# Three more 512-token blocks through the Strassen loop of a two-mixer kernel, with their combined weights formed beside attention

## The chip, the cores and the metric

One core of a Trainium2 chip runs the program. The metric is device microseconds of one execution. Before the change the median of three runs is 1919.4 us (1916.83 to 1920.06).

## What is computed

```python
# attention: q, k, v are (8, 8, 576, 64); k and v are averaged over 8 neighbours first
scores = q @ k_p.T / sqrt(64);  x = softmax(scores) @ v_p        # -> (8, 576, 512)
# first mixer: token mixing of rank 32, then a channel network 512 -> 2048 -> 512
u = x + (x.T @ U @ V).T
x = u + relu(u @ w_ch1) @ w_ch2
# second mixer: 2-D Fourier transform (real part), layer norm, a channel network of the same size
u = x + real(fft(fft(x, axis=1), axis=2))
out = u + relu(norm(u) @ w_ch1b) @ w_ch2b
```

There are 4608 tokens of 512 channels in 8 batches of 576. All is float32; every operand of a large product is split into a high and a low part, and a product is three matmuls (high by high, high by low, low by high).

## The kernel before

The two channel networks take nearly all of TensorE's time. Each has a first product (512 to 2048 channels, in 16 column blocks f of 128) and a second one (2048 back to 512).

**First mixer** (lines 1097 to 1171). Tokens come in groups of 256 (`T`); the first two run as a pair. For each f, `st1` (L879) makes one [128, 256] tile of the hidden layer and `st2` (L927) multiplies the tile of an earlier f by `W[1, f]`. One turn of the f loop is called a slot here; 18 groups of 16 slots cover all tokens, the first two groups sharing their slots. In each slot other work, written as Python generators ("lanes", L1017), moves on by a step: attention (`a`), the rank-32 mixing (`mix`), loads (`prep`), weights (`w`), operands of the next group (`p`), and the spectral work (`d`).

`st1` has two forms. As long as attention runs (no `Dft` object), a tile takes twelve 128x256 matmuls. Afterwards ("beside", L880) it takes four 128x512 and four 128x256 matmuls with the same number of columns in all.

**Weights.** The raw inputs are float64 bit patterns. `w_first` (L137) converts those of the first mixer to split float32 in `W[0, f]` and `W[1, f]`, with integer operations on VectorE (L124, L129, L130), copies on ScalarE and the subtraction of the split on GpSimd (L100). `w_second` (L177) does it for the second mixer's first matrix and forms the seven combinations of Strassen's scheme (Winograd's form) per pair of column blocks, splits them (`put`, GpSimd again) and stores them in the DRAM tile `wc`; then it converts the second matrix into `wd`. It uses a ring of four `wo` tiles.

**Second mixer** (lines 1207 to 1263). Blocks of 512 tokens (`TA`). For each of 8 pairs p of column blocks, seven `product` calls (L867) of six 128x256 matmuls each replace what would be eight; weights come in pairs through a ring of four slots (`ring_load`, L861, 512 KB each). `st2_a` (L957) is the second product. `prep_a` (L765) makes the operands of a block: it loads four tiles of 128 tokens from `u2d`, normalises them, transposes each with four TensorE matmuls against `ident` (L812) and splits. In the first mixer `turn_prep` (L707) transposes on VectorE instead. Four times in each p, `tick` (L1192) lets the spectral lane, the operands and `swap` move a step.

**Spectral work** (`Dft.run`, L523) handles one batch; the middle rows of several batches are gathered and handled together at the end of a group (`GROUPS`). It starts when all attention and weight lanes are done, runs beside the first mixer until its end and then beside the second, and writes `u2d`. `swap` (L1082) replaces `W[1, f]` by the second mixer's matrix, from the last 16 slots of the first mixer on.

What sets the order: up to the second mixer a scheduler of the language places the instructions of TensorE, VectorE, GpSimd and SyncE by its own estimates and the written order; an instruction whose inputs and buffers are free may be placed well ahead of where it is written. ScalarE keeps the written order from the second group on, TensorE and VectorE from the second mixer on. Every engine and the DMA queue of SyncE then work strictly in the order placed.

## Time and profile before

| | before |
|---|---|
| median of three runs | 1919.4 us |
| the profiled execution, its own time | 1924.2 us |
| its span, first to last instruction | 1922.4 us |
| mean granted TensorE clock | 0.989 |
| TensorE busy | 1840.7 us (96%) |
| VectorE busy | 1024.2 us (53%) |
| ScalarE busy | 676.6 us (35%) |
| GpSimd busy | 173.3 us (9%) |

Start times are in us from the span's start. The first mixer's matmuls begin at 65.7, attention and weight work end at 770, the spectral work runs from 772 to 1541, the second mixer's first product begins at 1088, and the last store is issued at 1919. Matmuls are pipelined, so the difference between the starts of two neighbouring groups, not a matmul's own duration, is what a group costs.

### The profile page before, as it was taken

To read this page: it belongs to the slowest core of one execution; us is meant where nothing else is said; L and a number is where in the kernel's file an instruction comes from. 1 tells how busy PE (TensorE), PEld (TensorE's weight loads), DVE (VectorE), ACT (ScalarE), POOL (GpSimd) and SP (SyncE) were. 2 spreads that over 40 slices of the span, in tenths; PEclk is the share of its full clock that TensorE was granted. 3 is DMA by queue.
4 is the path that set the end of the run, shared out by engine and by line. 5 is a ranking of instruction groups with operands and counts; after the bars stand their busy time and mean duration, and the time that the engine had idled before them with its cause. 6 is when DMAs were issued, how large, how long until landed. Compare 5 with 4: busy or idle time off the path is not lost. (4 is left out here: it accounts for less than half of the span.)

```text
span 1922.4 us, 30977 instructions
## 1 busy us (share of the span) xinstructions
PE 1840.7 (96%) x11252; PEld 1633.1 (85%) x11252; DVE 1024.2 (53%) x2365; ACT 676.6 (35%) x2116; POOL 173.3 (9%) x309
## 2 busy tenths in 40 slices
PE   4789899999999999999999899999999999999999
PEld 3578789898988888888888788899898999999998
DVE  8985464546454444545455855565656454445332
ACT  6553434343433332222232533333333323333221
POOL 3431011111100000100000100000000000000000
PEclk9799999999999999999999999999999999999999
DMA  9535464647453534422223767686768666666564
GB/s 362 173 115 176 134 196 141 196 129 214 120 184 110 144 105 136 131 78 63 77 64 99 247 195 223 214 260 208 223 223 265 201 223 191 229 185 225 182 212 132
DMA packets 255417, 335.63 MB, mean 175 GB/s; under 512 B 84576, under 2 KB 109248, under 8 KB 255264
## 3 DMA queue, kind: packets, MB, share of 16 engines
q1 hardware_dynamic: 254336, 330.25, 54.9%
q0 software_dynamic: 928, 3.40, 0.5%
q8 instruction: 89, 1.46, 0.3%
q14 instruction: 64, 0.52, 0.1%
HBM read 268.69 MB, written 64.88 MB: 174 GB/s over the span
## 5 line engine op out<-in xcount | busy, mean ns | idle before, releaser
L110 PE MATMUL h<-utx,w 128*128 128x256 f32 (+1 forms) x3048 | 479.6, 302 | 14.3 <-DVE hl L921 5.9
L110 PE MATMUL o<-w,hh 128*128 128x512 f32 x1632 | 478.8, 399 | 1.7 <-DVE ur L103 0.8
L110 PEld LDWEIGHTS h<-utx,w 128*128 128x128 f32 x3048 | 432.6, 192 | 55.3 <-DVE hl L921 9.3
L110 PEld LDWEIGHTS h<-x,wr 128*128 128x128 f32 x3024 | 396.2, 191 | 27.2 <-issue 4.8
L110 PE MATMUL h<-x,wr 128*128 128x256 f32 x3024 | 411.4, 284 | 5.9 <-DMA wr<-wc 3.6
L110 PEld LDWEIGHTS o<-w,hh 128*128 128x128 f32 x1632 | 289.4, 190 | 49.1 <-ACT hh L920 2.3
L110 PE MATMUL o<-w,hl 128*128 128x512 f32 x816 | 278.4, 398 | 2.5 <-DVE hl L921 1.6
L110 PEld LDWEIGHTS o<-w,hl 128*128 128x128 f32 x816 | 150.3, 190 | 29.1 <-DVE hl L921 2.9
L103 DVE TENSOR_TENSOR side<-h,side 128x256 f32<-128x256 f32 (+1 forms) x144 | 79.5, 552 | 116.7 <-PE h L110 116.1
L413 ACT ACTIVATE s<-s,mx 128x72 f32<-128x72 f32 x296 | 90.4, 332 | 70.6 <-DVE mx L410 70.1
L915 ACT ACTIVATE low<-h 128x256 f32<-128x256 f32 x102 | 39.1, 383 | 205.3 <-PE h L110 168.4
L1183 ACT ACTIVATE hh<-side 128x256 fp32r<-128x256 f32 (+1 forms) x144 | 75.0, 521 | 94.7 <-DVE side L103 93.3
L920 ACT ACTIVATE hh<-h 128x256 fp32r<-128x256 f32 x170 | 65.6, 386 | 97.3 <-PE h L110 88.8
L1183 ACT ACTIVATE hh<-h 128x256 fp32r<-128x256 f32 x72 | 27.6, 383 | 203.8 <-PE h L110 202.3
L1189 DVE SCALAR_TENSOR_TENSOR hl<-h,hh 128x256 fp32r<-128x256 f32 x72 | 30.4, 423 | 124.4 <-ACT hh L1183 123.3
L103 DVE TENSOR_TENSOR low<-h,low 128x256 f32<-128x256 f32 x102 | 42.9, 420 | 94.1 <-ACT hh L916 91.5
L1189 DVE SCALAR_TENSOR_TENSOR hl<-side,hh 128x256 fp32r<-128x256 f32 (+1 forms) x144 | 79.3, 551 | 22.8 <-ACT hh L1183 21.3
L921 DVE SCALAR_TENSOR_TENSOR hl<-h,hh 128x256 fp32r<-128x256 f32 x170 | 70.4, 415 | 34.6 <-ACT hh L920 34.1
L110 PE MATMUL m<-w,hh 128*128 128x512 f32 x304 | 83.6, 394 | 0.0
L110 PE MATMUL hu<-w,hh 128*128 128x512 f32 x288 | 78.6, 394 | 0.0
L100 POOL TENSOR_TENSOR wo<-wo 128x256 fp32r<-128x256 f32 x56 | 43.3, 784 | 325.9 <-ACT wo L106 309.0
L413 ACT ACTIVATION_READ_ACCUMULATOR s<-s,mx 128x1 f32 x296 | 64.5, 218 | 0.0
(254 smaller groups left out, 2346.0 us busy)
## 6 DMA issues: line engine op xcount, KB each, us to landing
wr<-wc SPq DMA_DIRECT2D x252, 512.0 KB
x<-x SPq DMA_DIRECT2D x56, 256.0 KB
wc<-wo SPq DMA_DIRECT2D x56, 256.0 KB
ur<-ud SPq DMA_DIRECT2D x36, 256.0 KB
x1d<-ur SPq DMA_DIRECT2D x36, 256.0 KB
ul<-u2d SPq DMA_DIRECT2D x36, 256.0 KB
ur<-u2d SPq DMA_DIRECT2D x36, 256.0 KB
out<-ur SPq DMA_DIRECT2D x36, 256.0 KB
```

The source lines that it names most:

```text
L100: eng.tensor_tensor(out=o, in0=a, in1=b, op=ALU.subtract)
L103: eng.tensor_tensor(out=o, in0=a, in1=b, op=ALU.add)
L110: nc.tensor.matmul(o, a, b, start=start, stop=stop, skip_group_check=True)
L413: nc.scalar.activation(out=s[:n, a], in_=v[:, k], func=ACTF.Exp, bias=mx[:n, a:a + 1], accum_out=sm[:n, a:a + 1])
L915: nc.scalar.activation(out=low, in_=o[:, T:2 * T], func=ACTF.Copy)
L920: nc.scalar.activation(out=hh, in_=p, func=ACTF.Relu)
L921: nc.vector.scalar_tensor_tensor(out=hl, in0=p, scalar=0.0, in1=hh.bitcast(F32), op0=ALU.max, op1=ALU.subtract)
L1183: nc.scalar.activation(out=hh[:, i], in_=c, func=ACTF.Relu)
L1189: nc.vector.scalar_tensor_tensor(out=hl[:, i], in0=c, scalar=0.0, in1=hh[:, i].bitcast(F32), op0=ALU.max, op1=ALU.subtract)
```

## The change

The first mixer's own loop ends after 12 groups of 256 tokens. The last three blocks of 512 tokens (`SB` = 6 to 8) go through the Strassen loop ahead of the second mixer's nine, in one sequence `seq` of twelve blocks; a phase number selects the source (`ud` or `u2d`), the destination (`x1d` or `out`), the combined weights (`wc[0]` or `wc[1]`), and whether there is a layer norm.

The new lane `w_combine` forms the first mixer's combinations from `W[0, f]`, which lies in SBUF already split: per pair p eight additions or subtractions of 128x256 on VectorE, four splits (ScalarE, GpSimd), seven stores of 256 KB; `w_second` comes after it, and the `w` lane gets two steps in every second slot. The exchange of `W[1, f]` moves into the Strassen loop, behind the last use by the third block. Spectral groups are four pairs of batches.

```diff
-GROUPS = ((0, 1, 2), (3,), (4, 5), (6, 7))
+GROUPS = ((0, 1), (2, 3), (4, 5), (6, 7))
+SB = 6
...
-    wc = dram.tile([7 * NPR, 128, 512], F32, name="wc")
+    wc = [dram.tile([7 * NPR, 128, 512], F32, name=f"wc{i}") for i in range(2)]
...
+    def w_combine(at):
+
+        def half(p, i, h):
+            return W[0, 2 * p + i].bitcast(F32)[:, :, 256 * h:256 * h + 256]
+
+        def plain(w, n):
+            nc.sync.dma_start(out=wc[0][n].rearrange("p (h x) -> p h x", h=2), in_=w)
+
+        def put(o, n):
+            split(o[:, 0], o[:, 1], o[:, 1].bitcast(F32), nc.gpsimd)
+            nc.sync.dma_start(out=wc[0][n], in_=o.bitcast(F32).rearrange("p h x -> p (h x)"))
+
+        for p in range(NPR):
+            z = 7 * p
+            w11, w12, w21, w22 = half(p, 0, 0), half(p, 1, 0), half(p, 0, 1), half(p, 1, 1)
+            ra, rb, t1, t2 = at.wo(), at.wo(), at.wo(), at.wo()
+            a, b, x, y = ra.bitcast(F32), rb.bitcast(F32), t1.bitcast(F32), t2.bitcast(F32)
+            add(nc.vector, a[:, 0], w11[:, 0], w11[:, 1])
+            add(nc.vector, a[:, 1], w12[:, 0], w12[:, 1])
+            plain(w11, z)
+            yield
+            add(nc.vector, b[:, 0], w22[:, 0], w22[:, 1])
+            add(nc.vector, b[:, 1], w21[:, 0], w21[:, 1])
+            plain(w22, z + 4)
+            yield
+            sub(nc.vector, x[:, 1], a[:, 1], a[:, 0])
+            sub(nc.vector, a[:, 1], b[:, 0], a[:, 1])
+            plain(w21, z + 6)
+            yield
+            sub(nc.vector, y[:, 1], b[:, 0], x[:, 1])
+            sub(nc.vector, b[:, 1], b[:, 1], y[:, 1])
+            yield
+            for o, n in ((t1, 1), (ra, 3), (t2, 2), (rb, 5)):
+                put(o, z + n)
+                yield
...
+    seq = [(0, b) for b in range(SB, NBA)] + [(1, b) for b in range(NBA)]
...
-            nc.sync.dma_start(out=us[t], in_=u2d[r0:r0 + 128, :])
-        ahead = 4 if b else 2
+            nc.sync.dma_start(out=us[t], in_=(ud, u2d)[phase][r0:r0 + 128, :])
+        first = i == 0
+        ahead = 2 if first else 4
...
+            src = wc[seq[2 * m // (7 * NPR)][0]]
...
-            nc.sync.dma_start(out=out[r0:r0 + 128, :], in_=r)
+            nc.sync.dma_start(out=(x1d, out)[phase][r0:r0 + 128, :], in_=r)
+            if not phase and t == 1:
+                state["x1"] = (b + 1) * TA
+        if t == 1 and seq[k] == (0, NBA - 1):
+            swapq.extend((2 * p, 2 * p + 1))
...
-    groups = [[0, 1]] + [[j] for j in range(2, NB)]
+    groups = [[0, 1]] + [[j] for j in range(2, 2 * SB)]
...
-                if "w" not in lanes and not second:
+                if "w" not in lanes and len(second) < 2:
+                    lanes["w"] = (w_combine, w_second)[len(second)](at)
                     second.append(1)
-                    lanes["w"] = w_second(at)
...
-                for name in ("p", "mix", "w", "prep"):
+                for name in ("p", "mix", "w", "prep", "w") if f % 2 else ("p", "mix", "w", "prep"):
...
-    for b in range(NBA):
-        begun = False
+    for k in range(len(seq)):
+        begun = k + 1 == len(seq)
```

How the built order changes is shown at three places.

VectorE at the start, between the conversions of the first mixer's weights (`scr<-wraw`) and the steps that end in the first mixing (`hst`); `wo` is the ring in which combinations are formed. Before:

```order
L433 TENSOR_TENSOR scr_134<-s_430,sm 128x512
L129 SCALAR_TENSOR_TENSOR scr_477<-wraw,scr_477 128x512 x2
L423 TENSOR_SCALAR sm<-sm 128x8
L130 SCALAR_TENSOR_TENSOR scr_477<-wraw,scr_477 128x512 x2
L424 RECIPROCAL sm<-sm 128x8
L124 TENSOR_SCALAR scr_509<-wraw 128x512 x2
L129 SCALAR_TENSOR_TENSOR scr_509<-wraw,scr_509 128x512 x2
L433 TENSOR_TENSOR scr_135<-o_459,sm 128x512
L130 SCALAR_TENSOR_TENSOR scr_509<-wraw,scr_509 128x512 x2
L100 TENSOR_TENSOR hst<-hu,hst 32x512
```

and with the change:

```order
L101 TENSOR_TENSOR wo<-wo 128x256
L372 TENSOR_REDUCE kp<-raw 128x72
L470 TENSOR_TENSOR scr_135<-s_431,sm 128x512
L460 TENSOR_SCALAR sm<-sm 128x8
L130 SCALAR_TENSOR_TENSOR scr_478<-wraw,scr_478 128x512 x2
L101 TENSOR_TENSOR wo<-wo 128x256 x2
L461 RECIPROCAL sm<-sm 128x8
L125 TENSOR_SCALAR scr_510<-wraw 128x512 x2
L131 SCALAR_TENSOR_TENSOR scr_478<-wraw,scr_478 128x512 x2
L101 TENSOR_TENSOR wo<-wo 128x256
L470 TENSOR_TENSOR scr_136<-o_460,sm 128x512
```

Four of the combining operations stand in this piece; eight stand ahead of `hst`, and 40 of all 64 ahead of the last `wraw` conversion.

GpSimd at the same place, where it makes the low parts of `w` and of `wo`. Before:

```order
L100 TENSOR_TENSOR w<-scr_453,w 128x512 x2
L100 TENSOR_TENSOR w<-scr_477,w 128x512 x2
L100 TENSOR_TENSOR w<-scr_509,w 128x512 x2
L100 TENSOR_TENSOR w<-cv,w 128x512
L100 TENSOR_TENSOR w<-scr_684,w 128x512
```

and with the change:

```order
L101 TENSOR_TENSOR w<-scr_454,w 128x512 x2
L101 TENSOR_TENSOR wo<-wo 128x256 x2
L101 TENSOR_TENSOR w<-scr_478,w 128x512
L101 TENSOR_TENSOR wo<-wo 128x256
L101 TENSOR_TENSOR w<-scr_478,w 128x512
L101 TENSOR_TENSOR wo<-wo 128x256
L101 TENSOR_TENSOR w<-scr_510,w 128x512 x2
```

Sixteen of the 32 new subtractions stand ahead of the last one of `w<-cv`.

TensorE, in the first spectral batches. Before, beside the first mixer's slots (`st`: table of the transform, `utx`: operands of 256 tokens):

```order
L110 MATMUL s_8726<-st,xh_8330 128x290 x2
L110 MATMUL s_8726<-st,xl_8331 128x290
L110 MATMUL h_8396<-utx,w 128x512
L110 MATMUL h_8396<-utx,w 128x256
L110 MATMUL h_8396<-utx,w 128x512
L110 MATMUL h_8396<-utx,w 128x256
L110 MATMUL h_8396<-utx,w 128x512
L110 MATMUL h_8396<-utx,w 128x256 x2
L110 MATMUL h_8396<-utx,w 128x512
L110 MATMUL o_8415<-w,hh 128x512 x2
```

and with the change, beside the Strassen loop with the first mixer's tokens (`wr`: ring of combined weights, `x`: combined operands):

```order
L111 MATMUL s_8763<-st,xh_8403 127x290 x2
L111 MATMUL s_8763<-st,xl_8404 127x290
L111 MATMUL s_8763<-st,S 127x290
L111 MATMUL h_8708<-x_8514,wr 128x256 x6
L111 MATMUL h_8709<-x_8517,wr 128x256 x6
L111 MATMUL s_8792<-st,xe_8247 96x290 x2
L111 MATMUL s_8792<-st,xe_8402 96x290 x2
L111 MATMUL s_8792<-st,xe_8589 64x290
L111 MATMUL h_8708<-x_8456,wr 128x256 x6
L111 MATMUL h_8709<-x_8383,wr 128x256 x6
```

In the whole program the order holds, before and now: `h<-utx,w` of 128x512 408 and 72 times, of 128x256 2640 and 2160 times; `h<-x,wr` 3024 and 4032 times; transposes `s<-ident,ul` 128 and 176 times.

## Rows read from the trace of the kernel before

**Rows 1.** Busy time by stretch; columns as in the first line.
```profile
core 0: us, PE busy (x) PEld busy (x) DVE busy (x) ACT busy (x) POOL busy (x), PEclk, DMA share, GB/s
0.00:200.00 200.00, 150.65 (x856) 125.81 (x857) 152.38 (x279) 102.81 (x333) 63.95 (x74) 0.92 0.60 202
200.00:770.00 570.00, 550.68 (x3510) 494.68 (x3509) 285.16 (x664) 217.25 (x848) 48.43 (x74) 0.99 0.51 152
772.00:1000.00 228.00, 227.54 (x1197) 194.78 (x1196) 114.66 (x268) 63.98 (x189) 15.05 (x41) 1.00 0.29 83
1000.00:1110.00 110.00, 103.73 (x566) 87.79 (x565) 74.47 (x191) 42.08 (x116) 10.70 (x22) 1.00 0.55 170
1200.00:1500.00 300.00, 297.95 (x1914) 270.21 (x1912) 172.18 (x426) 98.01 (x250) 23.56 (x69) 1.00 0.71 232
```
**Rows 2.** Timeline of PE, a slot beside the spectral work: start us, us, what.
```profile
902.37 1.57 PE L110 MATMUL h<-utx,w 128*128 128x512 f32 x8
903.78 0.62 PE L110 MATMUL o<-w,hl 128*128 128x512 f32 x2
```
**Rows 3.** Timeline of PE, a slot beside attention.
```profile
400.96 1.58 PE L110 MATMUL h<-utx,w 128*128 128x256 f32 x12
402.38 0.63 PE L110 MATMUL o<-w,hl 128*128 128x512 f32 x2
```
**Rows 4.** Timeline of PE in the Strassen loop, two products and a transpose.
```profile
1704.25 1.59 PE L110 MATMUL h<-x,wr 128*128 128x256 f32 x12
1705.68 1.09 PE L110 MATMUL o<-w,hh 128*128 128x512 f32 x4
...
1707.08 0.60 PE L812 MATMUL s<-ident,ul 128*128 128x128 f32 x4
1707.43 1.67 PE L110 MATMUL h<-x,wr 128*128 128x256 f32 x12
```
**Rows 5.** Busy time in pieces of 20 us at the start.
```profile
40.00:60.00 20.00, 10.48 (x38) 6.42 (x36) 18.31 (x27) 9.76 (x18) 9.34 (x7) 0.73 0.77 297
100.00:120.00 20.00, 15.67 (x79) 13.16 (x80) 19.08 (x31) 11.64 (x33) 10.49 (x7) 0.83 0.41 130
180.00:200.00 20.00, 17.52 (x114) 15.52 (x113) 6.53 (x14) 4.41 (x16) 0.00 (x0) 1.00 0.39 111
```
**Rows 6.** Timeline of DVE ahead of the first mixer's operands; in brackets idle time before.
```profile
53.03 0.69 DVE L100 TENSOR_TENSOR hst<-hu,hst 32x512 fp32r<-32x512 f32 x1 [1.60 <-ACT hst L474]
53.75 1.40 DVE L124 TENSOR_SCALAR cv<-wraw 128x512 int32<-128x512 int32 x1
...
57.71 0.41 DVE L124 TENSOR_SCALAR scr<-wraw 128x512 int32<-128x512 int32 x1
...
64.95 0.68 DVE L100 TENSOR_TENSOR utx<-h,utx 128x512 fp32r<-128x512 f32 x1
```
**Rows 7.** Timeline of PE, the first mixer's first matmuls.
```profile
65.68 1.65 PE L110 MATMUL h<-utx,w 128*128 128x256 f32 x6 [4.04 <-DVE utx L100]
```
**Rows 8.** Timeline of POOL beside rows 6.
```profile
53.59 1.27 POOL L100 TENSOR_TENSOR w<-scr,w 128x512 fp32r<-128x512 f32 x1 [0.76 <-ACT w L106]
```
**Rows 9.** Tile wo on DVE: ns min/median/max, first and last start us.
```profile
L100 DVE TENSOR_TENSOR wo<-wo x32: 380/416/559, 143.2 to 526.6; 128x256 f32<-128x256 f32 x32
```
**Rows 10.** Tile wo on POOL.
```profile
L100 POOL TENSOR_TENSOR wo<-wo x56: 725/740/1184, 143.8 to 532.9; 128x256 fp32r<-128x256 f32 x56
```
**Rows 11.** Tile wraw on DVE.
```profile
L129 DVE SCALAR_TENSOR_TENSOR scr<-wraw,scr x28: 671/680/1775, 21.5 to 124.6; 128x512 int32<-128x512 int32 x28
```
**Rows 12.** Groups of DVE, 30 to 130 us: busy us, mean ns | idle before.
```profile
L129 DVE SCALAR_TENSOR_TENSOR scr<-wraw,scr 128x512 int32<-128x512 int32 x24 | 21.3, 908 | 0.1
```
**Rows 13.** Groups of PE, 200 to 770 us.
```profile
L110 PE MATMUL hu<-xl,ust 128*128 128x512 f32 x30 | 13.1, 437 | 6.0 <-DVE xl L100 5.8
```
**Rows 14.** Groups of PE, 1000 to 1200 us.
```profile
L110 PE MATMUL h<-x,wr 128*128 128x256 f32 x386 | 53.3, 285 | 4.8 <-DMA wr<-wc 2.5 <-DVE side L103 1.4 <-ACT side L1230 0.5
L110 PE MATMUL h<-utx,w 128*128 128x512 f32 x224 | 44.3, 340 | 1.0 <-DVE low L103 1.0
```

More of the change, by code (lines that the diff above doesn't have):

```diff
@@ L814, in prep_a @@
                 load(t + ahead)
-            if b == 0:
+            if first:
                 if t % 2 == 0:
@@ L846, in prep_a @@
             yield
-            if b == 0:
+            if first:
                 for h, m in ((0, "s2"), (1, "s4")):
@@ L850, in prep_a, with late_op @@
                 yield
-        if b:
+        if not first:
             late_ops.update(s2=[quarter(r[i], 0) for i in range(2)], s4=[quarter(r[i], 1) for i in range(2)])
-    def late_op(b, m):
-        x = ops[b + 1][m] = optile()
+    def late_op(k, m):
+        x = ops[k + 1][m] = optile()
         for i, src in enumerate(late_ops.pop(m)):
@@ L879, in st1 @@
     def st1(js, f, tag):
-        beside = len(js) == 1 and df is not None
+        beside = len(js) == 1 and df
         o = bank(tag)
@@ L1076 @@
     hq = []
-    df = None
+    df = []
+    dbx = ExitStack()
     second = []
@@ L1084, in swap @@
         i = swapn[0]
-        if not swapq:
+        if i >= len(swapq) + (3 if len(swapq) == NF else 0):
             return
         swapn[0] += 1
-        for lag, fn in ((2, w_swap), (5, w_swap_split)):
+        for lag, fn in ((0, w_swap), (3, w_swap_split)):
             f = i - lag
@@ L1091, in swap, with spectral @@
                 fn(f)
-    groups = [[0, 1]] + [[j] for j in range(2, NB)]
+    def spectral():
+        if df or [name for name in lanes if name != "p"]:
+            return
+        abx.close()
+        df.append(Dft(dbx))
+        lanes["d"] = lane_d(df[0])
+    groups = [[0, 1]] + [[j] for j in range(2, 2 * SB)]
     late = []
@@ L1100 @@
         wide = len(js) > 1
-        last = js[-1] == NB - 1
+        last = js[-1] == 2 * SB - 1
         tags = (("o0", "o1"), ("h1", "m"))
@@ L1108 @@
             hs = st1(js, f, "h0" if one else "h1")
-            if last:
-                swapq.append(f)
-                if f >= NOP:
-                    ring_load(f - NOP)
+            if last and f >= NOP:
+                ring_load(f - NOP)
             if late and f == 4:
@@ L1165 @@
                 rest(js[0])
-            swap()
+    if not df:
+        until(lambda: not [name for name in lanes if name != "p"])
+        spectral()
     for js, f, hs in hq:
         st2(js[0], f, hs[0], ("o0", "o1"))
-        swap()
-    finish(NB - 1)
-    state["x1"] = NTOK
+    finish(2 * SB - 1)
+    state["x1"] = SB * TA
     state["banks"] = ("s0",)
@@ L1206 @@
     chain.enter_context(tc.manual_schedule(engines={mybir.EngineType.PE, mybir.EngineType.DVE}))
-    for b in range(NBA):
-        begun = False
+    for k in range(len(seq)):
+        begun = k + 1 == len(seq)
         for p in range(NPR):
-            x = ops[b]
-            n = 7 * (NPR * b + p)
-            end = p == NPR - 1 and b + 1 < NBA
-            begun = begun or begin(b)
+            x = ops[k]
+            n = 7 * (NPR * k + p)
+            end = p == NPR - 1 and k + 1 < len(seq)
+            if not begun and ready_for(k + 1):
+                begun = True
+                lanes["p"] = prep_a(k + 1)
             h0, h1 = bank("h0"), bank("h1")
```

78 lines of the change are left out of this document (36 added, 42 removed).

## The prediction

> **What bounds the kernel now.** I read the busy time by stretch first [rows 1]. TensorE is the bound from about 200 us on: it is idle for 19.3 of the 570 us beside attention (570 less 550.68), for 0.5 of the 228 us in which the first mixer runs beside the spectral work, for 6.3 of the 110 us around the change from the first mixer's loop to the Strassen loop, and for 2.1 of 300 us in the Strassen loop with spectral work beside it. [...] The first 200 us are another regime: there TensorE is busy for 150.65 us only. The pieces of 20 us [rows 5] show who is full instead: VectorE, with 18.31 of 20 us from 40 to 60 and 19.08 from 100 to 120; by 180 to 200 it has fallen to 6.53. The timelines show how this reaches TensorE. Just ahead of the first mixer's operands VectorE runs one operation after the other with a single pause of 1.60 us [rows 6], and TensorE's first matmul of that mixer starts at 65.68 after 4.04 us of waiting for them [rows 7]. So matmul time saved after 200 us is saved from the end; an operation more on VectorE before some 120 us can cost its full length; later it costs a share.
>
> **The matmuls.** The order gives the counts. The 128x512 form of `h<-utx,w` falls by 336, four to a slot, so 84 slots of the form beside the spectral work go; the 128x256 form falls by 480, of which 336 belong to those slots, and the other 144 are 12 slots of twelve. A first product beside the spectral work takes 903.78 - 902.37 = 1.41 us [rows 2], one beside attention 402.38 - 400.96 = 1.42 us [rows 3]: removed are 84 x 1.41 + 12 x 1.42 = 135.4 us. Added are 1008 matmuls `h<-x,wr`; twelve of them take 1705.68 - 1704.25 = 1.43 us [rows 4], so 84 x 1.43 = 120.1 us. The three blocks' operands are now transposed on TensorE, 48 matmuls more, and four take 1707.43 - 1707.08 = 0.35 us [rows 4]: 12 x 0.35 = 4.2 us. The second products have the same form and number in both loops. Net **-11.1 us**, all on the bounding engine. The saving is much smaller than the eighth that Strassen's scheme takes off, since the transposes eat a quarter of it.
>
> **The combined weights, at the start.** `w_combine` adds 64 VectorE operations of 128x256, 32 splits and 56 stores of 256 KB. It was written to follow the conversion of the weights, but the placed order has 40 of the 64 ahead of the last conversion, in the stretch in which VectorE is full, and eight ahead of `hst`, on the path to the first matmul of the mixer. One such operation takes 0.416 us [rows 9]. The eight take 3.3 us; the pause of 1.60 us [rows 6] can hide part: lower bound 1.7 us. If all 40 delay TensorE, the bound above is 40 x 0.416 = 16.6 us. A second price is the neighbour: `cv<-wraw` at 53.75 took 1.40 us where the same operation at 57.71 took 0.41 [rows 6], and it ended some 0.3 us after a GpSimd subtraction that began at 53.59 and took 1.27 [rows 8]; over the stretch the conversions L129 take 0.908 us in the mean [rows 12] against a median of 0.680 in the whole [rows 11], 0.2 us of stretching each. With 0.2 us more for each of the eight (1.6 us in all), the start comes to 3.3 + 1.6 - 1.6 = 3.3 us; the order also places two conversions L129, at 0.908 us [rows 12], ahead of `hst` that stood behind it, which if it counts makes 5.1. I take **+4 us**, nearer the lower bound than the upper, because of the other 32 the order places most behind the mixer's own `hl` and `hw` operations and ahead of attention's, and because VectorE is two thirds idle by 180 us [rows 5], so that attention's delay is made up before TensorE needs it. A gain is not excluded either, since the mixer's operations now stand earlier among the others: rival 4 has the term at nothing. [...]
>
> The ScalarE copies and the stores stay off the path: ScalarE is busy 102.81 of the first 200 us, and the transfers take 0.60 of the DMA engines' time there [rows 1]. On SyncE's queue each stored combination waits for a GpSimd subtraction (0.740 us [rows 10]), and what queues behind it are loads of later weights and of attention's next batch; that cover is gone only if a store waits for many microseconds, which would show as attention falling behind.
>
> **The rest beside attention.** 24 operations of 0.416 us are left, 10 us on a VectorE that is busy 285.16 of 570 us [rows 1]. TensorE's idle time there is latency: 5.8 us behind `xl` alone in 30 uses [rows 13]. If idle time grows with VectorE's load, it is 19.3 x 10 / 285 = 0.7 us; the denser steps of `w_second` add a little. **+1 us**, between 0 and 4.
>
> **Spectral work beside the Strassen loop.** A block takes 8 x (3.5 x 1.43 + 4 x 1.40) = 84.8 us, with 1707.08 - 1705.68 = 1.40 us for a quarter of the second product [rows 4]; three are 254 us. Idle share there 0.68%, beside the first mixer 0.2% [rows 1]: 254 x 0.48% = **+1.2 us**. The regrouping to four pairs leaves the number of gathered tails at four: nothing.
>
> **The change of loop and the exchange of W[1].** The waits at the change, 2.5 us for a ring load, 1.4 for VectorE's `side` and 1.0 for `low` [rows 14], keep their place but come earlier. The 16 exchanged matrices and their splits no longer fall on it; they go beside the third block. **0 us**: from -2.4 (the two waits for VectorE vanish) to +3.9 (one more ring wait and one more for `side`).
>
> **Sum.** -11.1 + 4 + 1 + 1.2 + 0 = -4.9 us. The profiled execution took 1924.2 us of its own and would take 1919.3; it stands 4.8 us above the median of the runs, 1919.4, which would be **1914.5 us**. About 0.2%, 3.8 us, is what a measurement of this kernel can tell from no change, so this is a gain just beyond it.
>
> **Rivals.**
> 1. *VectorE pays in full (slower).* All 40 early operations reach TensorE: -11.1 + 16.6 + 1 + 1.2 = +7.7, **1927.1 us**. It decides if TensorE's idle time in the first 200 us grows by more than 8.9 us. For it: VectorE at 95% from 100 to 120 us [rows 5]. Against: TensorE's own work of that stretch also waits for attention, which the order moves later. Chance 0.10.
> 2. *GpSimd holds VectorE (slower).* Sixteen new subtractions of 0.740 us [rows 10] stand in the full stretch; if each holds VectorE for its length, as 1.40 against 0.41 us shows for one conversion [rows 6, 8], 11.8 us are added to the lower bound of 1.7: -11.1 + 13.5 + 1 + 1.2 = +4.6, **1924.0 us**. Against: the combining operations that run beside such subtractions today take 0.559 us at most [rows 9]. Chance 0.08. [...]
> 3. *The exchange collides (no change).* Loads of the exchanged matrices join ring and spectral loads, where the DMA engines are already busy 0.71 of the time [rows 1]: +3.9 in place of 0, -1.0 in all, **1918.4 us**. Against: the exchange spreads over a whole block. Chance 0.25.
> 4. *The start is free (faster).* The combining operations fill time in which VectorE would wait, and the loop change sheds 2.4 us: -11.1 + 0 + 0 + 1.2 - 2.4 = -12.3, **1907.1 us**. Against: one pause of 1.60 us is all that rows 6 hold. Chance 0.15.
>
> That the change would not do what it says is excluded by the order: the counts above are those of three blocks moved.
>
> **How the numbers follow.** The forecast has 0.42, with a range of its own from 1910 to 1919; about 0.30 of it lies beyond 0.2%. With rival 4 and a little of rival 3 that makes faster 0.47; the rest of the forecast and most of rival 3 make the same 0.33; rivals 1 and 2 and a remainder of rival 3 make slower 0.20. The range from 1907 to 1927 ends at rivals 4 and 1 and leaves out the bounds beyond them.
>
> **What would show it.** Right: in the changed profile the start of the first `h<-utx,w` lies near 70 us, TensorE's idle time in the first 200 us is within some 6 us of 49.4 (200 less 150.65), the spectral work starts about twelve slots sooner than at 772 relative to the first mixer, twelve Strassen blocks of about 85 us plus spectral matmuls follow each other, and the last store comes some 5 us sooner. The forecast falls if VectorE stays full beyond 140 us and TensorE's idle time before 200 us exceeds 58 us; if ring loads (`wr<-wc`) end waits of over 5 us in sum beside the exchange; or if TensorE's idle time beside attention exceeds 25 us.

## The result and the profile after

The change makes the kernel slower: 1941.3 us (1937.0 to 1946.6, four runs) against 1919.7 us (1916.8 to 1923.3, four runs) of the kernel before on the same chip, ratio 1.0113 with a 95% interval from 1.0082 to 1.0143. The forecast was 1914.5 us and the range ended at 1927. The profiled execution of the changed kernel took 1941.2 us, 17.0 us more than that of before (1924.2).

The page of the changed kernel: its span, the busy time of the engines (instructions behind the x), the chain of work that ended last by line, and the two groups of first and second products that differ most from before (busy, mean ns of one | idle time before, releaser).

```profile
span 1939.4 us, 31791 instructions
PE 1840.9 (95%) x11492; PEld 1645.8 (85%) x11492; DVE 1049.6 (54%) x2411; ACT 702.0 (36%) x2154; POOL 196.8 (10%) x341
PE h L111 27%; PE o L111 17%; PE m L111 7%; PE hu L111 7%; DMA cv<-w2b 5%; PE s L111 4%; PE s L850 1%; DMA out<-ur 1%; DVE hl L960 0%; DVE cv L125 0%; DMA w<-wd 0%; SPq L742 0%; DMA x1d<-ur 0%; DVE cv L131 0%; DMA R<-x1d 0%
L111 PE MATMUL o<-w,hh 128*128 128x512 f32 x1440 | 418.9, 402 | 19.1 <-ACT hh L959 14.7
L111 PE MATMUL h<-utx,w 128*128 128x256 f32 (+1 forms) x2232 | 331.3, 293 | 12.1 <-DVE hl L960 5.3
```

TensorE is as busy as before and idle for longer. A transfer, `cv<-w2b`, holds 5% of the chain, and the second product `o<-w,hh` waits 14.7 us for ScalarE's relu `hh`. Busy time by stretch (columns as in [rows 1]) says where:

```profile
0.00:200.00 200.00, 146.65 (x806) 123.28 (x807) 153.33 (x284) 100.27 (x322) 74.01 (x83) 0.88 0.67 231
200.00:770.00 570.00, 534.63 (x3359) 476.89 (x3358) 301.30 (x705) 225.36 (x879) 67.78 (x97) 0.98 0.54 165
1587.00:1846.00 259.00, 259.00 (x1637) 233.72 (x1636) 115.65 (x282) 79.30 (x199) 7.71 (x12) 1.00 0.69 208
```

Beside attention TensorE is idle for 35.4 us of 570, where [rows 1] have 19.3; in the first 200 us for 53.4, where they have 49.4. Three Strassen blocks near the end, with no spectral work beside them, take 259 us, 86.3 each, with no idle time. To put places on the loss I count ScalarE's relus of the first mixer (tiles `hw`, `hh`), sixteen to a group of tokens. The 25th begins at 185.4 us (177.2 before), the 97th at 457.0 (445.9), the 121st at 545.1 (535.4), the 169th at 757.0 (722.2). So some 8 us are lost by 185 us, only 2 more by 545 us, and 25 us between 545 and 757.

**The late loss.** From 544 to 754 us the lane of the weights converts `w2b`, the second mixer's second matrix. Who waits for whom there (us in total, times, longest):

```profile
ACT cv L126 <- DVE cv L125: 91.6, 29, 7.1
DVE cv L125 <- DMA cv<-w2b: 81.8, 30, 4.8
PEld o L111 <- ACT hh L959: 14.9, 7, 3.5
PE o L111 <- ACT hh L959: 12.4, 5, 3.2
```

The timelines of SyncE's queue, VectorE, ScalarE and TensorE, 640 to 658 us, in this order (start us, us, what, in brackets the idle time before and its releaser):

```profile
639.41 0.68 SPq L281 DMA_DIRECT2D wd<-cv  x1
640.19 0.37 SPq L218 DMA_DIRECT2D cv<-w2b  x1
...
645.75 0.32 SPq L281 DMA_DIRECT2D wd<-cv  x1
646.17 0.37 SPq L218 DMA_DIRECT2D cv<-w2b  x1
...
643.79 0.29 DVE L125 TENSOR_SCALAR cv<-cv 128x256 int32<-128x256 int32 x1 [4.11 <-DMA cv<-w2b]
644.12 0.43 DVE L130 SCALAR_TENSOR_TENSOR cv<-cv 128x256 int32<-128x256 int32 x1
644.57 0.69 DVE L101 TENSOR_TENSOR hst<-hu,hst 32x512 fp32r<-32x512 f32 x1
...
645.75 0.77 DVE L960 SCALAR_TENSOR_TENSOR hl<-h,hh 128x256 fp32r<-128x256 f32 x2
...
650.22 0.29 DVE L125 TENSOR_SCALAR cv<-cv 128x256 int32<-128x256 int32 x1 [3.11 <-DMA cv<-w2b]
...
656.25 0.29 DVE L125 TENSOR_SCALAR cv<-cv 128x256 int32<-128x256 int32 x1 [3.40 <-DMA cv<-w2b]
656.46 0.68 DVE L104 TENSOR_TENSOR ur<-o,ur 128x512 f32<-128x512 f32 x1
...
644.17 0.44 ACT L126 ACTIVATE cv<-cv 128x256 f32<-128x256 f32 x1 [3.97 <-DVE cv L125]
644.50 0.37 ACT L959 ACTIVATE hh<-h 128x256 fp32r<-128x256 f32 x1
...
650.60 0.43 ACT L126 ACTIVATE cv<-cv 128x256 f32<-128x256 f32 x1 [4.54 <-DVE cv L125]
650.94 0.37 ACT L959 ACTIVATE hh<-h 128x256 fp32r<-128x256 f32 x1
...
644.93 1.20 PE L111 MATMUL o<-w,hh 128*128 128x512 f32 x4 [2.31 <-ACT hh L959]
...
657.29 0.78 PE L111 MATMUL o<-w,hh 128*128 128x512 f32 x2 [3.05 <-DVE ur L104]
```

The load is issued at 640.19 and lands 3.47 us later (the chain of waits gives its length as 3.47, 3.93 and 3.76 us for three in turn). VectorE's first operation on it, L125, stands ahead of `hst` and `hl` in VectorE's order, and all of them stand still for 4.11 us. ScalarE keeps the written order: its L126 needs L125, and the relu stands behind L126 and comes at 644.50. TensorE waits 2.31 us for that relu. Six microseconds later VectorE and ScalarE stand still again (3.11 and 4.54 us); this time TensorE has other matmuls and does not wait. At the load after that it waits again, 3.05 us, for an operation of VectorE (`ur`) that stands behind L125. In the whole trace of the change the 2411 operations of VectorE and the 1833 activations of ScalarE start in the order placed, line after line.

**The early loss.** Two pieces of 20 us of the change, of which the first answers to [rows 5], and then the second piece in the kernel before:

```profile
100.00:120.00 20.00, 13.33 (x65) 10.36 (x64) 19.94 (x31) 9.08 (x18) 9.09 (x9) 0.88 0.44 144
120.00:140.00 20.00, 16.30 (x91) 13.85 (x90) 20.00 (x38) 11.23 (x34) 11.27 (x9) 0.87 0.57 180
120.00:140.00 20.00, 18.45 (x118) 15.84 (x118) 14.59 (x28) 11.28 (x34) 5.43 (x5) 1.00 0.28 93
```

VectorE is full from 100 to 140 us; before, it had 19.08 of the first piece and 14.59 of the second, and TensorE 15.67 and 18.45. The relus place the loss more closely. The first matmul of the mixer comes 3.5 us late (69.19 against 65.68), yet the 11th relu begins at 112.9 us, 10.9 us earlier than before. The 17th begins at 156.3 us, 10.2 us later than before. So the early loss falls between 113 and 156 us; the change, and then the kernel before:

```profile
113.00:156.00 43.00, 31.92 (x157) 25.69 (x158) 38.02 (x69) 22.22 (x67) 21.21 (x16) 0.84 0.55 176
```

```profile
113.00:156.00 43.00, 40.91 (x255) 34.84 (x254) 32.00 (x63) 24.48 (x82) 15.13 (x15) 1.00 0.44 146
```

### The profile page after: what moved, and what is told of

It is laid out like the page before. It is cut to its first block, busy times and chain, and to the rows that moved or that the text cites. A ratio compares the mean times of both kernels' runs of the same rounds, so it can differ in the third digit from the quotient of the medians.

```text
span 1939.4 us, 31791 instructions
## 1 busy us (share of the span) xinstructions
PE 1840.9 (95%) x11492; PEld 1645.8 (85%) x11492; DVE 1049.6 (54%) x2411; ACT 702.0 (36%) x2154; POOL 196.8 (10%) x341
## 4 chain that ended last, share of the span: by engine, by line
PE 62%; DMA 8%; DVE 4%; issue 1%; ACT 1%; SPq 1%; DVEq 0%; POOL 0%; ACTq 0%; POOLq 0%
PE h L111 27%; PE o L111 17%; PE m L111 7%; PE hu L111 7%; DMA cv<-w2b 5%; PE s L111 4%; PE s L850 1%; DMA out<-ur 1%; DVE hl L960 0%; DVE cv L125 0%; DMA w<-wd 0%; SPq L742 0%; DMA x1d<-ur 0%; DVE cv L131 0%; DMA R<-x1d 0%
## 5 line engine op out<-in xcount | busy, mean ns | idle before, releaser
L111 PEld LDWEIGHTS h<-x,wr 128*128 128x128 f32 x4032 | 527.0, 190 | 25.6 <-DVE side L104 0.7
L111 PE MATMUL h<-x,wr 128*128 128x256 f32 x4032 | 547.8, 283 | 0.3
L111 PE MATMUL o<-w,hh 128*128 128x512 f32 x1440 | 418.9, 402 | 19.1 <-ACT hh L959 14.7
L111 PE MATMUL h<-utx,w 128*128 128x256 f32 (+1 forms) x2232 | 331.3, 293 | 12.1 <-DVE hl L960 5.3
L111 PEld LDWEIGHTS h<-utx,w 128*128 128x128 f32 x2232 | 308.0, 195 | 34.5 <-DVE hl L960 10.7
L104 DVE TENSOR_TENSOR side<-h,side 128x256 f32<-128x256 f32 x192 | 106.1, 553 | 137.9 <-PE h L111 137.1
L1230 ACT ACTIVATE hh<-side 128x256 fp32r<-128x256 f32 x192 | 99.9, 520 | 118.7 <-DVE side L104 115.3
L1236 DVE SCALAR_TENSOR_TENSOR hl<-side,hh 128x256 fp32r<-128x256 f32 x192 | 105.8, 551 | 27.9 <-ACT hh L1230 27.8
L450 ACT ACTIVATE s<-s,mx 128x72 f32<-128x72 f32 x296 | 90.5, 331 | 54.7 <-DVE mx L447 54.1
L111 PE MATMUL m<-w,hh 128*128 128x512 f32 x400 | 110.3, 395 | 0.0
L111 PEld LDWEIGHTS m<-w,hh 128*128 128x128 f32 x400 | 69.4, 191 | 9.4
L111 PEld LDWEIGHTS hu<-w,hh 128*128 128x128 f32 x384 | 66.0, 189 | 8.6
```

Source lines behind the costliest of these rows:

```text
L104: eng.tensor_tensor(out=o, in0=a, in1=b, op=ALU.add)
L111: nc.tensor.matmul(o, a, b, start=start, stop=stop, skip_group_check=True)
L450: nc.scalar.activation(out=s[:n, a], in_=v[:, k], func=ACTF.Exp, bias=mx[:n, a:a + 1], accum_out=sm[:n, a:a + 1])
L1230: nc.scalar.activation(out=hh[:, i], in_=c, func=ACTF.Relu)
L1236: nc.vector.scalar_tensor_tensor(out=hl[:, i], in0=c, scalar=0.0, in1=hh[:, i].bitcast(F32), op0=ALU.max, op1=ALU.subtract)
```

## The experiments

The theory: there are two losses, both of placement. In the late one VectorE is placed to stand before a transfer, with ScalarE's relu behind it, and the second `w` step of every odd slot makes this frequent. In the early one the combining, which needs no transfer, is placed ahead into the time in which VectorE is full. The rivals: the added operations themselves are too much there (density), or SyncE's queue is. Each kernel was timed beside the kernel before on one chip, and the ratio is to that; from session to session the kernel before took 1919.4 to 1924.0 us, so kernels are to be compared by their ratios, not by the column of times. "The words" are the first part of `w_second`, which converts `w1b` and forms the combinations in `wc`; the `w2b` part follows it.

| run | edit | us | ratio, 95% interval |
|---|---|---|---|
| the change | | 1941.3 | 1.0113, 1.0082 to 1.0143 |
| e1 | `w2b` loaded ahead | 1931.9 | 1.0038, 1.0023 to 1.0053 |
| e13 | ScalarE first in `w2b` | 1948.3 | 1.0143, 1.0127 to 1.0158 |
| e5 | both | 1906.7 | 0.9923, 0.9904 to 0.9942 |
| e3 | combining from group 2 | 1945.8 | 1.0109, 1.0090 to 1.0129 |
| e4 | e1 and e3 | 1919.6 | 0.9976, 0.9965 to 0.9988 |
| n1 | e5 without combining's arithmetic | 1898.5 | 0.9881, 0.9866 to 0.9896 |
| e6 | words first, then combining | 1932.3 | 1.0059, 1.0041 to 1.0078 |
| e7 | e5 and e6 | 1906.1 | 0.9916, 0.9898 to 0.9935 |
| e11 | e5, words rewritten | 1904.0 | 0.9911, 0.9893 to 0.9929 |
| e9 | e7, words rewritten | 1894.3 | 0.9861, 0.9846 to 0.9876 |
| e12 | e9, five tiles `wo` | 1898.1 | 0.9885, 0.9871 to 0.9900 |
| b1 | before, double `w` step | 1954.9 | 1.0162, 1.0146 to 1.0179 |
| b2 | before, `w2b` as in e5 | 1905.4 | 0.9919, 0.9900 to 0.9939 |
| b3 | b2, words rewritten | 1903.8 | 0.9908, 0.9894 to 0.9923 |
| b4 | b2, double `w` step | 1917.4 | 0.9975, 0.9964 to 0.9987 |

### The conversion of w2b: four corners

**e1, loads ahead** (`cols` lists the pieces; two are loaded ahead of the loop):

```diff
-            raw = load(w2b[f][:, c])
-            t = at.cv()[:, 0:256].bitcast(I32)
-            yield
+            raw = ahead.pop(0)
+            t = raw_of(at.wo()).bitcast(I32)
             high(raw, 256, t)
             yield
             nc.sync.dma_start(out=wd[f][:, c], in_=bits(raw, 256, t))
+            if i + 2 < 2 * NF:
+                f, c = cols[i + 2]
+                ahead.append(load(w2b[f][:, c]))
+            yield
```

> The change with one edit: in the last part of w_second (the conversion of w2b) each raw half is loaded two pieces ahead and the converted word goes into a tile wo, so that a load and its high (L125) no longer fall into the same slot; the number of steps a slot and the arithmetic stay. Theory A (VectorE waits in its order for a load issued in the same slot, ScalarE in its written order waits behind it, and with it the relu that TensorE needs): the stretch from 573 to 781 us gets its some 20 us back, about 1921 us, and VectorE's waits for the load of w2b fall from 81.8 us to under 20. Rival B (VectorE or ScalarE simply has too much work there with three steps per two slots): about 1940 us, TensorE's idle time in 600 to 780 us stays near 22 us. Rival C (the DMA queue of SyncE is what is full: 64 loads and stores between those of attention): within 5 us of 1941, with other loads late in place of it.

Measured 1.0038: about 14 of the expected 20 us came back. VectorE's waits, 548 to 746 us, missed the expectation by far:

```profile
DVE wo L125 <- DMA cv<-w2b: 72.4, 28, 4.2
```

The wait of L126 for L125 had all but gone from ScalarE (3.0 us in two), so the relus were free again; VectorE still stood before its loads, though each was now issued two pieces ahead. So the theory was wrong in one point: what counts for VectorE is not the slot in which L125 is written. Its order is the scheduler's, and an operation whose inputs are expected may be placed ahead of where it is written; as I read it, the load is expected sooner, and L125 moves up with it. The trace of e1 shows that it did. The load of one piece, its L125, and then the last operation (L131) of the piece before it:

```profile
640.66 0.37 SPq L218 DMA_DIRECT2D cv<-w2b  x1
...
644.11 0.29 DVE L125 TENSOR_SCALAR wo<-cv 128x256 int32<-128x256 int32 x1 [3.71 <-DMA cv<-w2b]
...
645.61 0.43 DVE L131 SCALAR_TENSOR_TENSOR wo<-cv,wo 128x256 int32<-128x256 int32 x1
```

In e1 L125 stands ahead of that L131 in 28 of 31 pieces, in the change in none, and it begins a median of 3.4 us after its load is issued, hardly less than in the change (3.6). Next, VectorE is made unable to stand before the load.

**e5, loads ahead and ScalarE first.** ScalarE's operation has a place fixed by the written order. If VectorE's depend on it, they can't be placed ahead of it:

```diff
-            high(raw, 256, t)
+            nc.scalar.activation(out=e, in_=hw.bitcast(F32), func=ACTF.Abs, scale=F64_BIAS)
             yield
-            nc.sync.dma_start(out=wd[f][:, c], in_=bits(raw, 256, t))
+            nc.vector.tensor_scalar(out=t, in0=e.bitcast(I32), scalar1=3, scalar2=None, op0=ALU.logical_shift_left)
+            nc.vector.scalar_tensor_tensor(out=t, in0=lw, scalar=29, in1=t, op0=ALU.logical_shift_right, op1=ALU.bitwise_or)
+            nc.vector.scalar_tensor_tensor(out=t, in0=hw, scalar=-0x80000000, in1=t, op0=ALU.bitwise_and, op1=ALU.bitwise_or)
+            nc.sync.dma_start(out=wd[f][:, c], in_=t.bitcast(F32))
```

> The change with the w2b part of w_second written anew: loads two pieces ahead, and ScalarE's operation on a piece comes first, into a tile of its own; VectorE's three operations depend on it, so VectorE can't be placed to wait for the load itself any more. The steps a slot and the number of operations stay. Theory A (what was lost at 573 to 781 us is VectorE standing in its order before a load that the chip delivers later than the order supposes): VectorE's waits for w2b go from 72 us (with the loads ahead) to under 10, and the rest of the loss comes back too: some 10 us under the kernel with the loads ahead, ratio to the kernel before about 0.999. Rival B (what is left there is the number of operations): the same as with the loads ahead, ratio about 1.004. Rival C (now ScalarE stands before the load, and the relu behind it): slower than that, ratio 1.008 or more.

Measured 0.9923, 22 us better than e1 where I expected 10, and 14 us under the kernel before. The waits listed for VectorE and ScalarE from 545 to 723 us hold none for `w2b`. With the same number of operations and steps, density is out for this loss.

**e13, ScalarE first, loads as in the change:**

```diff
             yield
-            high(raw, 256, t)
+            nc.scalar.activation(out=hw.bitcast(F32), in_=hw.bitcast(F32), func=ACTF.Copy, scale=F64_BIAS)
             yield
...
```

> The change with ScalarE first in the w2b part, but each piece loaded when it was in the change, in the step ahead, not two pieces ahead. With the loads ahead alone the ratio was 1.0038, with both 0.9923, with neither 1.0113. Theory A (an engine in its written order must not stand before a load): now ScalarE stands before the load and the relu behind it, TensorE waits for hh as in the change; 1.005 to 1.015. Rival (it was VectorE's place alone, ScalarE has the time): 0.992 to 0.997.

Measured 1.0143, at the upper end of theory A. The waits from 565 to 790 us:

```profile
ACT cv L279 <- DMA cv<-w2b: 117.6, 31, 6.8
PEld o L111 <- ACT hh L962: 33.6, 19, 4.3
PE o L111 <- ACT hh L962: 27.6, 17, 4.0
```

Now ScalarE itself stands before the load and the relu behind it. Loads ahead alone bring back 14 us, ScalarE first alone costs 6 more, and together they bring back 36. (The corners are not quite alike: ScalarE's result goes into a tile of its own in e5, and stays in place in e13.)

### The same loss in the kernel before

**b1, the kernel before with the double step alone:**

```diff
-                for name in ("p", "mix", "w", "prep"):
+                for name in ("p", "mix", "w", "prep", "w") if f % 2 else ("p", "mix", "w", "prep"):
```

> The kernel before with one line of the change alone: two steps of the weights' lane in each odd slot (no combining for the first mixer, no Strassen blocks of it, spectral groups as they were). Theory A (two steps in one slot put a load of w2b and the operation that waits for it together): the part that converts w2b loses TensorE time here too, some 15 to 20 us, about 1937 us. Rival B (the loss comes from what else the change has there, fewer slots or the longer lane): 1920 us within 3, since the same work is only done earlier.

Measured 1.0162, 31 us, more than the whole change loses. The stretch in which it converts `w2b`, 384 to 600 us, in b1 and then in the kernel before:

```profile
384.00:600.00 216.00, 188.61 (x1122) 166.13 (x1121) 110.32 (x263) 72.63 (x289) 8.98 (x16) 0.93 0.55 159
```

```profile
384.00:600.00 216.00, 210.22 (x1348) 189.47 (x1347) 111.57 (x256) 86.58 (x344) 23.15 (x35) 0.99 0.52 156
```

VectorE is no busier in b1 (110.3 against 111.6 us), and TensorE has 21.6 us less of busy time, without a further Strassen block and without combining. TensorE waits 14.0 us for the relu `hh` there, in seven times; in the kernel before it has no such wait from 200 to 770 us.

**b2, the kernel before with the conversion of `w2b` as in e5,** nothing of the change.

> The kernel before with the w2b part written anew in the same way (loads two pieces ahead, ScalarE first), and nothing of the change. It tells what of the gain of such a version belongs to the Strassen blocks. Theory A: VectorE waited 83 us for w2b there too, but in slots of its own, with ScalarE's relu not behind it, so little comes back: ratio 0.997 to 1.000. Rival (those waits cost the kernel before as well): ratio 0.993 or less, and then the better versions owe it to this alone.

Measured 0.9919: the rival held. The kernel before pays some 16 us for these waits too. Its stretch from 510 to 770 us, in the kernel before and then in b2:

```profile
510.00:770.00 260.00, 248.66 (x1563) 221.83 (x1562) 122.22 (x297) 88.09 (x335) 8.80 (x16) 0.99 0.47 137
```

```profile
510.00:770.00 260.00, 258.94 (x1661) 234.94 (x1661) 131.97 (x308) 91.95 (x346) 12.16 (x23) 1.00 0.52 152
```

So e5 beat the kernel before for a reason that has nothing to do with Strassen blocks, and every later version had to be judged against b2 as well.

**b4, b2 with the double step.**

> The kernel before with the w2b part rewritten (ScalarE first) and two steps of the weights' lane in each odd slot. The doubled step without that rewriting gave 1.0162, the rewriting alone 0.9919. Theory A (the doubled step hurt by putting load and waiting operation together): most of the difference of 31 us goes, ratio 0.992 to 0.997, and what is left falls in the twelve words, which still have the old form. Rival B (denser steps cost by their work): 1.005 or more.

Measured 0.9975, just past the range of theory A. The kernel before, b1, b2 and b4 form a square, and it tells where the late loss comes from. The old conversion of `w2b` costs against the new one 16 us with single steps (1 less 0.9919), and 36 with the double step (1.0162 less 0.9975). In the change, which has the double step too, it costs 36 (1.0113 less 0.9923). So what the change loses there beyond the kernel before is what the double step makes of that conversion, and neither the Strassen blocks nor the combining is needed for it.

With the new conversion the double step still costs 11 us. By the 73rd relu, before the conversion of `w2b` begins, b4 is 13.0 us behind b2 (369.9 and 356.9); in 177 to 400 us VectorE waits for tiles `wo` still being stored (`DMA wc<-wo`, 21.4 us in 12), in the words, which keep the old form. ScalarE too waits for `w2b` again, 38.9 us in 12. That these waits make up the 11 us is argued here; for the words, e9 tests it.

### The start

**e3, combining from the second group on:**

```diff
-                if "w" not in lanes and len(second) < 2:
+                if gi and "w" not in lanes and len(second) < 2:
```

> The change with one edit: w_combine begins with the second group of the first mixer's loop, from which on ScalarE keeps the written order, so its operations can't be placed ahead among the first blocks. Theory A (the early place costs: VectorE is full until 140 us, and what the first blocks need of it comes late): the first h<-utx,w begins near 66 us instead of 69.2, the loss of 11 us by 150 us falls to 3 or less, about 1933 us in all. Rival B (the combining costs the same wherever it stands beside attention): the loss only moves behind 150 us, 1941 us within 3. Rival C (the lane of the weights ends some ten slots later, so the spectral work begins later and is late for the Strassen loop): 1945 us or more, with TensorE idle at the change of loop.

Measured 1.0109, no gain. The early loss did go: the 25th relu begins at 173.4 us, 12 us earlier than in the change. But the lane ends later, the spectral work's first matmul begins at 868.6 us in place of 796.3, and TensorE is idle for 11.9 us from 780 to 870 us, around the change of loop, where the change has 2.1: theory A at the place, rival C in the sum.

**e4, e1 and e3 together.**

> Both edits of the two runs before it in one kernel: w2b loaded two pieces ahead, and w_combine begun with the second group. Theory A (two separate losses, some 20 us at the w2b part and some 8 us at the start): about 1912 us, which is under the kernel before (1919.7). If the two rivals hold (density of work, not place and waits): about 1940 us. If only the w2b part is a matter of waits: about 1920 us.

Measured 0.9976, some 3 us less of a gain than expected. The spectral work's first matmul again begins late, at 843.6, and VectorE still waits 54.7 us for `w2b`; what each of the two takes is not shown.

**n1, e5 without the combining's arithmetic.** Its eight VectorE operations and four splits per pair are left out; all seven stores stay and take halves of `w`:

```diff
-            for o, n in ((t1, 1), (ra, 3), (t2, 2), (rb, 5)):
-                put(o, z + n)
+            for w, n in ((w12, 1), (w11, 3), (w22, 2), (w21, 5)):
+                plain(w, z + n)
                 yield
...
```

> The change with the w2b part rewritten (ratio 0.9923), and without the arithmetic of w_combine: its steps and its 56 stores stay, but every store takes a half of w as it is, so the first mixer's last blocks multiply by other weights. It prices the combining's operations on VectorE, ScalarE and GpSimd beside the first blocks. Theory A (they cost TensorE some 8 to 10 us, whatever their busy time elsewhere): ratio 0.987 or 0.988, and by 185 us no later than the kernel before. Rival (the stores or the steps cost, not the arithmetic): 0.991 to 0.993.

Measured 0.9881, 8 us under e5: the arithmetic, not stores or steps, is what costs at the start. The 17th relu begins at 136.6 us (155.8 in e5), the 25th at 176.3 (184.9). Of these 8.6 us only 2.9 are left at the 121st, so the 8 us of the whole are not simply the early loss carried through; where the rest comes back is open.

**e6, another order of the lane** (with the `w2b` part made a lane of its own, `w_down`):

```diff
-                if "w" not in lanes and len(second) < 2:
-                    lanes["w"] = (w_combine, w_second)[len(second)](at)
+                if "w" not in lanes and len(second) < 3:
+                    lanes["w"] = (w_second, w_combine, w_down)[len(second)](at)
```

> The change with the lane of the weights in another order: the twelve combined words of w_second first (as in the kernel before), then w_combine, then the w2b part; nothing else. The lane is as long as in the change. Theory A (combining without loads, placed ahead among the first blocks, is what costs at the start): by 185 us some 8 us earlier than the change, and no later start of the spectral work, so about 8 us less in all, ratio to the kernel before about 1.007. Rival (the combining costs the same wherever it stands): 1.011 as the change. The loss in the w2b part stays in both.

Measured 1.0059, in line with theory A, yet not cleanly: the 25th relu begins at 179.0 us, 6 earlier than in the change, but the 73rd is as late as there (367.9 against 366.7). What the combining no longer loses, the words lose a little later, with their waits and the double step.

**e7, e5 and e6 together.**

> Both edits of the two runs before it: the words first, then the combining, then the w2b part with loads ahead and ScalarE first. Theory A (two losses, both of placement): ratio to the kernel before about 0.995, some 10 us under it, which is then close to the sum that the matmul count alone gives. Rival (density): no better than the better of the two alone, 1.00 to 1.005.

Measured 0.9916, no better than e5 and b2 alone. Its waits from 177 to 370 us name what is left: ScalarE 23.1 us for L125 of the words, L125 19.9 us for tiles `wo` (`DMA wc<-wo`). From 540 us on ScalarE, which now comes first, waits 27.8 us for `w2b`, in ten times.

**e9, e7 with the words rewritten like w2b,** with ScalarE's result in place:

```diff
-            high(raw, 256, t)
+            nc.scalar.activation(out=hw.bitcast(F32), in_=hw.bitcast(F32), func=ACTF.Copy, scale=F64_BIAS)
             yield
-            bits(raw, 256, t)
+            nc.vector.tensor_scalar(out=t, in0=hw, scalar1=3, scalar2=None, op0=ALU.logical_shift_left)
...
```

> The kernel with the words first, then the combining, then the w2b part with ScalarE first (ratio 0.9916), and the same rewriting in the twelve-word part of w_second: ScalarE's operation first, in place, VectorE's three behind it. Theory A (every conversion whose first VectorE operation waits for its load itself costs TensorE time): by 366 us the loss against the kernel before falls from 9.6 us to under 4, ratio about 0.987. Rival B (there VectorE waits for tiles wo still being stored, not for loads: 19.9 us, DMA wc<-wo): the same ratio, 0.990 to 0.993. Rival C (ScalarE stands before the load of w1b, the relu behind it): 0.995 or more.

Measured 0.9861: 1894.3 us, 27 us under the kernel before and by the ratios some 48 under the change. It is the best version, with the double step and every added operation in it, so density is not what makes the change slow. The rewriting of the words brings 11 us against e7, and the lateness of the 73rd relu against the kernel before fell from 9.6 to 3.0. The waits are not all gone: ScalarE stands before `w2b` for 28.8 us, in ten times, up to 6.6. But TensorE waits only 2.2 us for a relu `hh` from 200 to 770 us, where the change has 13.9.

**b3, the kernel before with both conversions rewritten.**

> The kernel before with ScalarE first in both parts of w_second, nothing of the change. Theory A: VectorE waited there for tiles wo only some 7 us in 177 to 357 us, so little is left to gain: ratio 0.990 to 0.993, as with the w2b part alone (0.9919). Rival: the words cost as much as w2b did: 0.985.

Measured 0.9908 as expected. It is the fair neighbour of e9: what lies between them is the change (with the words first), with most of the waits taken out of both. It is worth 9.5 us (1903.8 and 1894.3 us on one chip).

**e11, e9 in the change's order of the lane** (combining first).

> The change in its own order of the lane (combining first, then the words, then w2b) with ScalarE first in both conversions; against the kernel with the words first (ratio 0.9861) only the order differs. Theory A (the combining placed ahead among the first blocks still costs there, whatever the conversions do): 7 to 9 us more, ratio 0.990 to 0.991, and 7 us or more late by 185 us. Rival (the order is of no account once the conversions don't hold VectorE): 0.986.

Measured 0.9911, 9.6 us behind e9, and 7.4 late by the 25th relu (184.6 and 177.2). The early loss is the place of the combining, and stays when the conversions are mended.

**e12, e9 with five tiles `wo`:**

```diff
-            return self.p.tile([128, 2, 256], F32R, tag="wo", name="wo", bufs=4)
+            return self.p.tile([128, 2, 256], F32R, tag="wo", name="wo", bufs=5)
```

> The kernel with the words first and ScalarE first in both conversions (ratio 0.9861), with five tiles wo in place of four. Theory A (VectorE's and ScalarE's places are settled; waits for a tile wo still being stored are short now): 0.985 to 0.987. Rival (the ring of four still holds VectorE): 0.983 or less.

Measured 0.9885, at the wrong side of both: no gain, rather some 5 us worse, though the two intervals just overlap. Why is left open. VectorE's waits for tiles `wo` from 177 to 800 us are much the same (25.4 us, 28.1 in e9), so one tile more does not take them away; a longer ring was not tried.

## Why the prediction was wrong

The runs split the difference of 21.6 us, by the ratios times 1919.7 us. The old conversions cost the change 38.8 us (1.0113 less 0.9911) and the kernel before 17.7 (1 less 0.9908), so 21.1 more. The place of the combining costs 9.6 (0.9911 less 0.9861). The rest of the change brings -9.0 (0.9861 less 0.9908). The parts add up by the way they are taken, so their sum proves nothing; each by itself is uncertain by 3 to 7 us.

1. **The matmuls, the spectral work and the loop change: right as a sum.** Without the start, the forecast had -11.1 + 1 + 1.2 + 0 = -8.9; e9 against b3 has -9.0. That the two agree so closely is luck, given the uncertainty. The largest term has a check of its own: TensorE is busy for 1834.9 us in b3 and for 1823.5 in e9, 11.4 less, at mean granted clocks of 0.988 and 0.990. The three Strassen blocks of 259 us are the 254 that were worked out and the 4.2 of their transposes, which the prediction counts elsewhere. No run measured the other terms one by one.
2. **The rest beside attention, +1 between 0 and 4: the step that failed.** It says "the denser steps of `w_second` add a little". The two conversions took 21 us more than in the kernel before, nearly all in `w2b`, where the square of b1, b2 and b4 puts it down to the double step; no run of the change itself leaves that step out. I costed the added operations by VectorE's busy share and did not ask which instruction waits there, and what stands behind it. The trace of before had the row. From 510 to 770 us, the kernel before:

```profile
DVE cv L124 <- DMA cv<-w2b: 83.2, 30, 5.4
ACT cv L125 <- DVE cv L124: 57.7, 20, 6.3
```

   Instead I read TensorE's groups [rows 13], where `xl` came first with 5.8 us, and took idle time for latency that grows with load. That these waits already cost the kernel before some 16 to 18 us, b2 and b3 had to show.
3. **The start, +4: sized at less than half, and in part at the wrong place.** e11 against e9 gives 9.6, n1 against e5 8.1, inside the bounds of 1.7 and 16.6. What I priced came as priced: with eight operations ahead of `hst` the first matmul came 3.5 us late. But that was more than made up by the 11th relu, and the loss fell between 113 and 156 us, among the other 32 operations, which I set at nothing because "attention's delay is made up before TensorE needs it". It was not: 8 us by the 25th relu are 11 at the 97th. The signs that I named did hold, the first matmul at 69.19 us and idle time up by 4.0, and were too weak: the trace counts 806 matmuls in the first 200 us instead of 856, and at a lower granted clock (0.88 against 0.92) a part of that counts as busy time.
4. **Rival 2 was partly true.** I argued from 32 operations of 0.559 us at most that GpSimd does not hold the combining. That was a misreading: only one of the 32 began while a GpSimd operation of two inputs (TENSOR_TENSOR) ran, and that one did wait: it took 0.56 us, the other 31 took 0.43 at most. VectorE, then GpSimd, in the kernel before:

```profile
146.77 0.56 DVE L100 TENSOR_TENSOR wo<-wo 128x256 f32<-128x256 f32 x1 [0.97 <-DMA wc<-wo]
...
146.32 0.72 POOL L100 TENSOR_TENSOR wo<-wo 128x256 fp32r<-128x256 f32 x1 [1.80 <-ACT wo L106]
```

   and in the change:

```profile
108.09 1.40 DVE L104 TENSOR_TENSOR wo<-w 128x256 f32<-128x256 f32 x1
...
107.92 1.28 POOL L101 TENSOR_TENSOR w<-scr,w 128x512 fp32r<-128x512 f32 x1 [0.38 <-ACT w L107]
```

   Both ended 0.28 us after the GpSimd operation that had begun ahead of them. In the change ten of the 96 operations began while such a GpSimd operation ran; seven of the ten ended 0.28 us after it and took 0.72 to 1.51 us, while the other three, and the 86 that began beside none, took 0.43 at most. The seven were stretched by some 5.5 us in all, so it is not the 11.8 us of that rival: most of the operations never met GpSimd.
5. **The condition of falling** that I wrote down, idle time beside attention over 25 us, was met: 35.4. No rival had the mechanism, so the range could not reach it.

## What to carry to other kernels

Ask the profile for the waits of every engine, not of the bounding one alone: in the change VectorE, busy for 54% of the span, waited 3.11 us up to 650.22 at no cost to TensorE, and 4.11 us up to 643.79, with the relu behind it, at a cost of 2.31 us. What such a wait cost depended on whether something that TensorE needed was placed behind it. Where a planner orders one engine and the text another, make the first operation on a transfer belong to the engine with the fixed place, and load far enough ahead of it; here loads ahead alone brought back 14 of 36 us, and the order alone made it worse. And when a mended version beats the kernel before, put the mend into the kernel before too: 18 of e9's 27 us were never the change's.

## What was not expected of the hardware

The granted clock took part in the price: its mean was 0.982 in the change and 0.990 in e9. From 660 to 675 us the change, and then e9:

```profile
660.00:675.00 15.00, 11.83 (x65) 10.37 (x64) 6.85 (x16) 2.98 (x8) 0.00 (x0) 0.85 0.64 172
```

```profile
660.00:675.00 15.00, 15.00 (x100) 13.70 (x100) 7.36 (x21) 6.90 (x31) 0.00 (x0) 1.00 0.41 124
```

In the change TensorE was idle for 3.17 us of this stretch, in one wait for the relu `hh`, and the granted clock was 0.85; in e9 it had no pause, and the clock was 1.00. Not every stretch with pauses shows it: from 615 to 630 us the change had TensorE busy for 11.18 us at a clock of 1.00. Where the clock was lower, the same matmuls took longer: in the change four `o<-w,hh` of 128x512 took 660.00 - 658.29 = 1.71 us, at a clock of 0.50 from 658 to 661 us, and 640.55 - 639.63 = 0.92 us at one of 1.00 from 639 to 642 us. Both kernels run 11492 matmuls. The page counts 1840.9 us of busy TensorE for the change and this for e9:

```profile
span 1891.8 us, 31847 instructions
PE 1823.5 (96%) x11492; PEld 1636.6 (87%) x11492; DVE 1049.8 (55%) x2411; ACT 701.1 (37%) x2154; POOL 198.3 (10%) x341
```

So 17.4 of the 47.6 us between the two spans lie in busy time and not in idle time: idle time alone understated what the waits cost.
